# Routed experts on 37 token tiles instead of 38: two shared tiles divided at 96

## The chip, the cores and the metric

The kernel runs on one core of one Trainium2 chip. The metric is the device time of one execution in microseconds (us); lower is better. A core has TensorE (PE; PEld is its weight load), VectorE (DVE), ScalarE (ACT), GpSimd (POOL) and a queue for plain transfers (SP). They run side by side and wait for each other by semaphores.

## The reference

Two blocks in a row, all in fp32: sliding attention, and a layer of 8 experts in which each token goes to one expert. Cut to what matters here:

```python
B, H, S, Dh = 8, 8, 576, 64          # 8 x 576 = 4608 tokens, D = 8 x 64 = 512
E, F = 8, 1024                       # 8 experts, hidden width 1024
attn = softmax(mask(q @ k.T / sqrt(Dh))) @ v          # window 32; half the heads dilated by 4
x = attn.transpose(0, 2, 1, 3).reshape(B, S, 512)
logits = x @ w_gate                                   # [B, S, 8]
local  = sigmoid(x @ w_local)
for b in range(B):
    for s in range(S):
        fresh = argmax(logits[b, s])
        e = fresh if s == 0 or local[b, s] < 0.5 else prev_e    # keep the expert of the token before
        prev_e = e
        h = relu(x[b, s] @ w1[e])                     # w1[e]: 512 x 1024, the first product
        out[b, s] = softmax(logits[b, s])[e] * (h @ w2[e])      # w2[e]: 1024 x 512, the second; times the gate
```

Which tokens an expert gets is known only at run time. The kernel computes each expert on its own tokens alone, gathered into tiles of 128.

## The kernel before

The first 137 us or so are attention; the router's work lies in its gaps. Once the first two of four groups of two batches are routed, 11 early tiles are formed from whole 128s of an expert; when all four are routed, the rest. 4608 tokens are 36 tiles of 128, but no expert has a multiple of 128: the remainder of an expert goes into a whole tile of its own if it is over 64, and into half of a shared tile if not. A shared tile has two positions, so two experts' weights. Three extra tiles run only if the counts ask for it.

```python
CAP = N // P                       # 4608 / 128 = 36
HALF = P // 2
EARLY = -(-(GROUPS[0] * GS - E * (P - 1)) // P)           # 11
FULL, MIXED, EXTRA = CAP - EARLY, 2, 3                    # 25 plain late tiles, 2 shared, 3 extra
# order: 11 early, a shared one, 25 plain (two chains of experts in turn), the other shared one; extras
...
# table(), the late part: which expert gets how many tiles and where its remainder begins
nc.vector.tensor_scalar(big, rest, float(HALF), None, Alu.is_gt)
nc.vector.scalar_tensor_tensor(small, rest, 0.0, big, Alu.is_gt, Alu.subtract)
...
def hidden(t, half):               # first product: h = relu(w1.T x), four of eight blocks m at a time
    hp = bank([P, FK // 2, P], "hp")
    to = by_half(hp, 1)[:, 0]
    for m in range(FK // 2):
        at = half * FK // 2 + m
        if len(ps) > 1:            # a shared tile: 64 weight columns by 64 tokens
            for swap in range(2):
                for kk in range(DK):
                    for u, p in enumerate(ps):
                        h = (u + swap) % 2 * HALF
                        nc.tensor.matmul(to[h:h + HALF, u, m], lhsT=w1s[p % 2][:, at, kk, h:h + HALF],     # L901
                                         rhs=x[:, kk, u * HALF:(u + 1) * HALF], ..., tile_position=(0, h))
        else:
            for kk in range(DK):
                nc.tensor.matmul(hp[:, m], lhsT=w1s[ps[0] % 2][:, at, kk], rhs=x[:, kk], ...)              # L907
    nc.scalar.activation(ht[t][:, half * FK // 2:(half + 1) * FK // 2], hp, Act.Relu)                      # L911

def output(t):                     # second product, and the gate
    yp = bank([P, D], "yp")
    for m in range(FK):
        if len(ps) > 1:
            for u, p in enumerate(ps):
                nc.tensor.matmul(yp[u * HALF:(u + 1) * HALF], lhsT=halves[:, m // (FK // 2), u, m % (FK // 2)],  # L931
                                 rhs=w2s[p % 2][:, m], ..., tile_position=(0, u * HALF))
        else:
            nc.tensor.matmul(yp, lhsT=h[:, m], rhs=w2s[ps[0] % 2][:, m], ...)                              # L935
        if go and m % 2 == 0:
            gather(t + 3, m // 2)  # tokens of the tile after next but one, by GpSimd (L860)
    y = mp.tile([P, D], F32, name="y")
    nc.vector.tensor_scalar(y, yp, of_tile("gate", t), None, Alu.mult)                                     # L943
    nc.gpsimd.indirect_dma_start(out=out, ..., in_=y)                                                      # L944

def weights(t, second, c):         # a quarter (512 KB) of w1 or w2 of a position, left out if the buffer
    cond = {} if t < 2 else dict(cond=ev[t] != ev[t - 2], cond_hint=False)      # already has this expert
    nc.sync.dma_start(out=s[t % 2][:, c * m:(c + 1) * m], in_=w[ev[t], c], **cond)
```

There are two buffers of weights, taken in turn by position. Between the first and the second product of a tile, TensorE transposes the gathered tokens of the next one (L877), and DVE copies them from PSUM (L879). `put` (L770) are products that turn the places of the tokens into the list of each tile; pv (L429) and sc (L376) are attention's, lp (L481) is the router's. Between matmuls, calls of `gap` (cut here) let waiting steps of the router and the list-making be put into TensorE's order.

Of the kernel before, what the change touches and what calls it, by code (L numbers as in the profile page):

```python
# [69 lines left out]

GROUPS = (2, NG)
EARLY = -(-(GROUPS[0] * GS - E * (P - 1)) // P)
FULL, MIXED, EXTRA = CAP - EARLY, 2, 3
COLS = (EARLY, FULL + MIXED + EXTRA)


# [18 lines left out]
C_ROW = C_GO + E * (NJ + 1)  # L97
C_AT = C_ROW + EARLY + FULL + 2 * MIXED + EXTRA
C_NUM = C_AT + FULL + 2 * MIXED + EXTRA
C_PAY = C_NUM + P  # L100
C_ALL = C_PAY + NG * NJ * TW


def plan():


    tiles = [[0, i // 2 + i % 2 * (EARLY - EARLY // 2), 1] for i in range(EARLY)]
    tiles += [[1, FULL, 2]]
    tiles += [[1, i // 2 + i % 2 * (FULL - FULL // 2), 1] for i in range(FULL)]
    tiles += [[1, FULL + i, 2] for i in range(1, MIXED)]  # L110
    tiles += [[1, FULL + MIXED + i, 1] for i in range(EXTRA)]
    end = 0
    for tile in tiles:
        tile[2] = tuple(range(end, end + tile[2]))
        end = tile[2][-1] + 1
    return tiles
# [9 lines left out]
def constants():  # L126

    c = np.zeros((P, C_ALL), np.float32)
    c[:, C_ID:C_TRI] = np.eye(P)
    c[:TB, C_TRI:C_IDX] = np.triu(np.ones((TB, TB)), 1)  # L130
    c[:, C_IDX:C_REV] = np.arange(E)
    c[:, C_REV:C_CODE] = E - np.arange(E)
    c[:TB, C_CODE:C_GO] = (np.arange(NJ)[None] * TB + np.arange(TB)[:, None]) * CW + E
    c[:, C_GO:C_ROW] = (np.arange(E * (NJ + 1)) % (NJ + 1) > 0)

    for lv, col, ps in TILES:
        for u, p in enumerate(ps):
            c[:, C_ROW + p] = N if len(ps) > 1 else col - MIXED * (col > FULL)
            if lv:
                c[:, C_AT + p - EARLY] = col * P + u * HALF  # L140
    c[:, C_NUM:C_PAY] = np.arange(P)
    s = np.arange(NG * NJ)[None] * TB + np.arange(TB)[:, None]
    pay = np.zeros((TB, NG * NJ, TW), np.float32)
    pay[:, :, 0] = s - N
    at = s % S
    for w, at in ((2, at), (3, at % DIL * CI + at // DIL)):
        pay[:, :, w] = ((s // S * 2 + w - 2) * P + at % QB) * NB + at // QB - ROWS
    c[:TB, C_PAY:] = pay.reshape(TB, -1)
    return c
# [126 lines left out]
def whole(ctx, tc, exact, qk, v, wgl, w1, w2, con, msk, qmk, out, cst, wg, ones, xd, kept, register):  # L276
# [322 lines left out]
    def table(lv):  # L599
# [7 lines left out]
        def by_expert(name):  # L607
            return new([P, E], name)
# [7 lines left out]
        nc.vector.tensor_copy(full, ni)  # L616
        if late:

            rest, big, small = by_expert("rest"), by_expert("big"), by_expert("small")
            nc.vector.scalar_tensor_tensor(rest, full, -float(P), cn, Alu.mult, Alu.add)  # L620
            nc.vector.tensor_scalar(big, rest, float(HALF), None, Alu.is_gt)
            nc.vector.scalar_tensor_tensor(small, rest, 0.0, big, Alu.is_gt, Alu.subtract)
            full_then = by_expert("full_then")
            nc.vector.tensor_tensor(full_then, full, tiles["done"], op=Alu.subtract)
            nc.vector.tensor_tensor(full, full_then, big, op=Alu.add)
        end = by_expert("end")
        nc.vector.tensor_tensor_scan(end, full, full, 0.0, Alu.add, Alu.max)
        start = by_expert("start")
# [11 lines left out]
        if not late:  # L640
# [10 lines left out]
            return  # L651
        tiles["first", lv] = first = by_expert("first")
        nc.vector.tensor_scalar(first, tiles["done"], float(P), None, Alu.mult)

        upto, number = by_expert("upto"), by_expert("number")
        nc.vector.tensor_tensor_scan(upto, small, small, 0.0, Alu.add, Alu.max)
        nc.vector.tensor_tensor(number, upto, small, op=Alu.subtract)
        total = end[:, E - 1:]
        nc.vector.tensor_scalar(number, number, total, None, Alu.add)
        most = new([P, 1], "most")  # L660
        nc.vector.tensor_scalar(most, total, float(FULL), None, Alu.max)
        half, begin = by_expert("half"), by_expert("begin")
        nc.vector.tensor_scalar(half, number, most, None, Alu.subtract)

        nc.vector.tensor_scalar(begin, half, float(HALF), float(FULL * P), Alu.mult, Alu.add)
        nc.vector.tensor_scalar(number, number, float(P), None, Alu.mult)
        nc.vector.tensor_tensor(begin, begin, number, op=Alu.min)
        nc.vector.tensor_scalar(half, half, 2.0 * MIXED, None, Alu.is_ge)
        nc.vector.scalar_tensor_tensor(number, number, -float(MIXED * P), begin, Alu.add, Alu.subtract)
        nc.vector.tensor_tensor(number, number, half, op=Alu.mult)  # L670
        nc.vector.tensor_tensor(begin, begin, number, op=Alu.add)

        nc.vector.tensor_scalar(full_then, full_then, float(P), None, Alu.mult)
        tiles["off_half", lv], tiles["from", lv] = off_half, since = by_expert("off_half"), by_expert("since")
# [2 lines left out]
        nc.vector.tensor_tensor(since, since, full_then, op=Alu.add)  # L677

        nc.vector.tensor_tensor(small, small, cst[:, C_IDX:C_REV], op=Alu.mult)
        nc.vector.tensor_tensor(ge, begin[0:1].unsqueeze(1).to_broadcast(shape),  # L680
                                cst[0:1, C_AT:C_AT + nt].unsqueeze(2).to_broadcast(shape), op=Alu.is_equal)
        nc.vector.tensor_tensor(ge, ge, small[0:1].unsqueeze(1).to_broadcast(shape), op=Alu.mult)
# [2 lines left out]
        none = new([1, nt], "none")  # L685
        nc.vector.tensor_scalar(none, er, float(E), -float(E), Alu.is_ge, Alu.mult)
        nc.vector.tensor_tensor(er, er, none, op=Alu.add)
        nc.vector.tensor_tensor(experts, er, eh, op=Alu.add)

        over, all_tiles = new([1, 1], "over"), new([1, 1], "all_tiles")  # L690
        nc.vector.tensor_tensor(over, total[0:1], upto[0:1, E - 1:], op=Alu.add)
        nc.vector.tensor_tensor(over, over, most[0:1], op=Alu.subtract)
        nc.vector.tensor_scalar(over, over, -2.0 * MIXED, 0.0, Alu.add, Alu.max)
        nc.vector.tensor_tensor(all_tiles, over, most[0:1], op=Alu.add)
        nc.vector.tensor_scalar(kept["number"], all_tiles, float(LAST - FULL), None, Alu.add)
        known[0] = POS

# [47 lines left out]
    def mark(lv, g):  # L745

        nt = COLS[lv]
        by_place = marks.tile([TB, NJ, P], F32, name="by_place")
        shape = [TB, NJ, P]
        nc.vector.tensor_tensor(by_place, cst[:TB, C_NUM:C_PAY].unsqueeze(1).to_broadcast(shape),  # L750
                                tiles["place"][:, g].unsqueeze(2).to_broadcast(shape), op=Alu.is_equal)
        shape = [TB, NJ, nt]
        there = sm.tile([TB, NJ, max(COLS)], F32, name="there")[:, :, :nt]
        nc.vector.tensor_tensor(there, cst[:TB, C_NUM:C_NUM + nt].unsqueeze(1).to_broadcast(shape),
                                tiles["tile"][:, g].unsqueeze(2).to_broadcast(shape), op=Alu.is_equal)
        by_tile = marks.tile([TB, NJ, loads(lv), nt], F32, name="by_tile", tag="by_tile", bufs=1)
        for w in range(loads(lv)):
            nc.vector.tensor_tensor(by_tile[:, :, w], there, pay[:, g, :, w].unsqueeze(2).to_broadcast(shape),
                                    op=Alu.mult)
        tiles["marks"] = by_place, by_tile  # L760
# [122 lines left out]

    def hidden(t, half):

        x, ps = xe[t], TILES[t][2]
        if not half:
            ht[t] = mp.tile([P, FK, P], F32, name="h")
        for p in ps:
# [2 lines left out]
        to = by_half(hp, 1)[:, 0]  # L892
        for m in range(FK // 2):
            at = half * FK // 2 + m
            if len(ps) > 1:

                for swap in range(2):
                    for kk in range(DK):
                        for u, p in enumerate(ps):
                            h = (u + swap) % 2 * HALF  # L900
                            here[:] = [nc.tensor.matmul(  # L901
                                to[h:h + HALF, u, m], lhsT=w1s[p % 2][:, at, kk, h:h + HALF],
                                rhs=x[:, kk, u * HALF:(u + 1) * HALF], start=(kk == 0), stop=(kk == DK - 1),
                                tile_position=(0, h), skip_group_check=True)]
            else:
                for kk in range(DK):
                    here[:] = [nc.tensor.matmul(hp[:, m], lhsT=w1s[ps[0] % 2][:, at, kk], rhs=x[:, kk],  # L907
                                                start=(kk == 0), stop=(kk == DK - 1))]
            if m < FK // 2 - 1:
                gap(0.9)  # L910
        nc.scalar.activation(ht[t][:, half * FK // 2:(half + 1) * FK // 2], hp, Act.Relu)  # L911
        if half:
            hid.update(ps)
            fetch(at_once[0])

    def by_half(h, n):

        return h.rearrange("p m q -> p (m q)").rearrange("p (a u m q) -> p a u m q", a=n, u=2, q=HALF)

    def output(t):  # L920
# [4 lines left out]
        go = t + 3 < min(LAST, named[0]) and not any(a <= t + 3 < a + 3 for a in (0, EARLY))  # L925
        halves = by_half(h, 2)
        for m in range(FK):
            if len(ps) > 1:

                for u, p in enumerate(ps):  # L930
                    here[:] = [nc.tensor.matmul(yp[u * HALF:(u + 1) * HALF], lhsT=halves[:, m // (FK // 2), u, m % (FK // 2)], rhs=w2s[p % 2][:, m],  # L931
                                                start=(m == 0), stop=(m == FK - 1), tile_position=(0, u * HALF),
# [7 lines left out]
            else:  # L940
                gap(0.9)
        y = mp.tile([P, D], F32, name="y")
        nc.vector.tensor_scalar(y, yp, of_tile("gate", t), None, Alu.mult)  # L943
        nc.gpsimd.indirect_dma_start(  # L944
            out=out, out_offset=bass.IndirectOffsetOnAxis(ap=of_tile("tok", t), axis=0),
            in_=y, in_offset=None, bounds_check=N - 1, oob_is_err=False)
# [15 lines left out]
    def route(g):  # L962
# [4 lines left out]
        lv = GROUPS.index(g + 1) if g + 1 in GROUPS else None  # L967
        if lv is not None:
            steps.insert(5, (0.0, lambda g: table(lv)))
            steps.append((1.2, lambda g: seek(lv)))  # L970

        waiting.extend((us if g + 1 == GROUPS[0] else 2 * us, lambda f=f: f(g)) for us, f in steps)
# [149 lines left out]
```

## Time and profile before

| | |
|---|---|
| time, three executions | 719.64 us median; 718.02 and 1607.11 the others |
| profiled execution | 713.95 us, span 712.2 us, granted TensorE clock 0.995 |
| tiles of the experts | 38: 36 plain, 2 shared |
| first and second product of plain tiles (L907, L935) | 265.0 and 255.0 us busy |
| first and second product of shared tiles (L901, L931) | 15.7 and 14.2 us busy |
| gathers (L860), two kinds of 76 | 973 and 948 ns on GpSimd on the mean, 2.7 us to landing (median) |

The span is what the profile covers, from the first to the last instruction of one execution; the time is of other executions and takes in a little more. An "x" gives the number of records; one fp32 matmul leaves two of them, each with its weight load. The chain of work that ended last is followed back from the last instruction: each piece is what the next one waited for.

```profile
L860 POOL DMA_INDIRECT xg<-xd,plain x76 | 74.0, 973 | 290.1 <-PE yp L935 243.9
L911 ACT ACTIVATE h<-hp 128x512 f32<-128x512 f32 x76 | 45.4, 597 | 499.6 <-PE hp L907 471.6
L943 DVE TENSOR_SCALAR y<-yp,gate 128x512 f32<-128x512 f32 x38 | 28.5, 751 | 212.1 <-DMA xg<-xd,dilated 92.7
```

A line of the groups has the source line, engine, operation, tile written and read, and count; then the busy time in us and the mean of one in ns; then how long the engine stood idle before it, and for whom.

### The profile page before, as it was taken

How to read it: one execution, taken by the hardware profiler on the slowest of the kernel's cores; microseconds unless marked ns; L12 is line 12 of the kernel's file. 1: busy time of each engine (PE TensorE's matmuls, PEld its weight loads, DVE VectorE, ACT ScalarE, POOL GpSimd, SP SyncE). 2: the span in 40 equal slices, each digit the busy share in tenths (PEclk: the TensorE clock that was granted, in tenths of full speed). 3: DMA queues.
4: the chain of work that ended last, by engine and by line, in shares of the span. 5: the costliest groups of instructions: out<-in, count | busy, mean ns of one | idle time of the engine just before them, and what ended most of it. 6: DMA issues, size and time to landing. Idle time of an engine off the chain costs nothing.

```text
span 712.2 us, 16720 instructions
## 1 busy us (share of the span) xinstructions
PE 695.4 (98%) x6460; PEld 527.5 (74%) x6460; DVE 194.8 (27%) x554; ACT 125.1 (18%) x241; POOL 211.2 (30%) x219
## 2 busy tenths in 40 slices
PE   8999989999999999999999999999999999999995
PEld 6989788876777777776677767776777667776772
DVE  4668797632257221001010101010100101010100
ACT  3565545412110000110001100110000000110010
POOL 2322200542223335203332333223332333233100
PEclk9999999999999999999999999999999999999998
DMA  9989779931864842807692451811178117201780
GB/s 340 384 278 341 244 265 396 392 139 31 295 237 148 287 136 53 273 25 260 197 319 72 134 170 38 270 38 34 38 256 291 35 37 240 73 31 38 228 295 15
DMA packets 37591, 131.24 MB, mean 184 GB/s; under 512 B 6686, under 2 KB 6814, under 8 KB 37504
## 3 DMA queue, kind: packets, MB, share of 16 engines
q1 hardware_dynamic: 29600, 110.68, 43.6%
q0 software_dynamic: 7904, 19.41, 9.7%
q8 instruction: 53, 0.87, 0.5%
q14 instruction: 34, 0.28, 0.1%
HBM read 207.37 MB, written 19.69 MB: 319 GB/s over the span
## 4 chain that ended last, share of the span: by engine, by line
PE 94%; DVE 4%; ACT 1%; issue 0%; POOL 0%; POOLq 0%; DVEq 0%
PE hp L907 36%; PE yp L935 35%; PE sc L376 6%; PE pv L429 4%; PE tp L877 2%; PE tp L455 2%; PE hp L901 2%; PE yp L931 2%; DVE pr L383 1%; PE lp L481 1%; PE put L770 1%; PE idle L341 1%; DVE x L435 1%; ACT pr L386 0%; ACT xt L466 0%
## 5 line engine op out<-in xcount | busy, mean ns | idle before, releaser
L907 PEld LDWEIGHTS hp<-xe,w1s 128*128 128x128 f32 x2304 | 263.3, 192 | 18.3 <-issue 16.3
L907 PE MATMUL hp<-xe,w1s 128*128 128x128 f32 x2304 | 265.0, 276 | 1.3 <-DVE xe L879 1.3
L935 PE MATMUL yp<-w2s,h 128*128 128x512 f32 x576 | 255.0, 594 | 0.0
L935 PEld LDWEIGHTS yp<-w2s,h 128*128 128x128 f32 x576 | 106.2, 190 | 118.0 <-issue 117.6
L860 POOL DMA_INDIRECT xg<-xd,plain x76 | 74.0, 973 | 290.1 <-PE yp L935 243.9
L911 ACT ACTIVATE h<-hp 128x512 f32<-128x512 f32 x76 | 45.4, 597 | 499.6 <-PE hp L907 471.6
L860 POOL DMA_INDIRECT xg<-xd,dilated x76 | 72.1, 948 | 57.1 <-PE yp L935 51.4
L943 DVE TENSOR_SCALAR y<-yp,gate 128x512 f32<-128x512 f32 x38 | 28.5, 751 | 212.1 <-DMA xg<-xd,dilated 92.7
L879 DVE COPY xe<-tp 128x512 f32<-128x512 f32 x38 | 26.2, 690 | 216.8 <-PE tp L877 216.8
L944 POOL DMA_INDIRECT out_dram<-y,tok x38 | 38.9, 1022 | 79.8 <-DVE y L943 78.8
L376 PE MATMUL sc<-kq 64*96 64x64 f32 x1152 | 57.2, 248 | 3.2 <-DVE pr L383 2.0
L376 PEld LDWEIGHTS sc<-kq 64*96 64x96 f32 x1152 | 52.2, 162 | 6.7 <-DVE pr L383 2.2
L383 DVE SCALAR_TENSOR_TENSOR pr<-sc,mk 96x640 f32<-96x640 f32 x64 | 47.8, 749 | 26.8 <-PE pv L429 15.6
L386 ACT ACTIVATE pr<-pr 96x640 f32<-96x640 f32 x64 | 43.6, 684 | 53.9 <-DVE pr L383 51.2
L332 POOL COPY vt<-vt 32x1040 f32<-32x1040 f32 x25 | 26.1, 1045 | 67.7 <-DMA vt<-in_v_dram 57.5
L429 PE MATMUL pv<-vt,pr 96*64 96x65 f32 x1152 | 43.6, 227 | 0.5 <-ACT xt L466 0.5
L429 PEld LDWEIGHTS pv<-vt,pr 96*64 96x64 f32 x1152 | 37.7, 139 | 6.5 <-issue 3.0
L435 DVE TENSOR_TENSOR x<-pv,rec 128x320 f32<-128x320 f32 x64 | 27.0, 454 | 0.2
L877 PE MATMUL tp<-cst,xg 128*128 128x128 f32 x152 | 23.0, 274 | 0.0
L455 PE MATMUL tp<-cst,x 128*128 128x128 f32 x144 | 20.3, 288 | 1.5 <-DVE x L435 1.4
L466 ACT COPY xt<-tp 128x288 f32<-128x288 f32 (+2 forms) x48 | 18.3, 557 | 1.9 <-PE tp L455 1.7
L455 PEld LDWEIGHTS tp<-cst,x 128*128 128x128 f32 x144 | 16.3, 146 | 2.7 <-DVE x L435 1.8
(178 smaller groups left out, 223.5 us busy)
## 6 DMA issues: line engine op xcount, KB each, us to landing
w1s<-in_w_dram SPq DMA_DIRECT2D x160, 512.0 KB
w2s<-in_w_dram SPq DMA_DIRECT2D x160, 512.0 KB
kq<-in_qk_dram SPq DMA_DIRECT2D x32, 592.0 KB
vt<-in_v_dram SPq DMA_DIRECT2D x32, 292.5 KB
xd<-x SPq DMA_DIRECT2D x16, 576.0 KB
xg<-xd,plain POOLq DMA_INDIRECT x76, 2.7
xg<-xd,dilated POOLq DMA_INDIRECT x76, 2.7
out_dram<-y,tok POOLq DMA_INDIRECT x38, 4.7
```

The costliest lines, as they stand in the source:

```text
L376: here[:] = [nc.tensor.matmul(sc[:KW, u, (i - a) * QB:(i - a + 1) * QB], lhsT=kt[h, i * QB:i * QB + KW], rhs=qt[h, i * QB:(i + 1) * QB], s ...
L383: nc.vector.scalar_tensor_tensor(pr[:, :, :w], sc[:KW, :, :w], -CEIL, mk[:, at:at + w].unsqueeze(1).to_broadcast([KW, 2, w]), Alu.max, Alu ...
L386: nc.scalar.activation(pr[:, :, :w], pr[:, :, :w], Act.Exp, scale=SCALE)
L429: here[:] = [nc.tensor.matmul(pv[u * QB:(u + 1) * QB, i - a], lhsT=pr[:, u, (i - a) * QB:(i - a + 1) * QB], rhs=vt[:, u, i], start=True, s ...
L435: nc.vector.tensor_tensor(x[:, a:z, n % 2], pv[:, :, :DH], r.unsqueeze(2).to_broadcast([P, z - a, DH]), op=Alu.mult)
L455: nc.tensor.transpose(tp[:, :, i], x[:, c * w + i].rearrange("p g d -> p (g d)"), ident)
L860: i = nc.gpsimd.indirect_dma_start(out=xg[t][:, kk], out_offset=None, in_=xd if full == ROWS else xd[:full], in_offset=bass.IndirectOffset ...
L877: nc.tensor.transpose(tp[:, kk], x[:, kk], ident)
L907: here[:] = [nc.tensor.matmul(hp[:, m], lhsT=w1s[ps[0] % 2][:, at, kk], rhs=x[:, kk], start=(kk == 0), stop=(kk == DK - 1))]
L911: nc.scalar.activation(ht[t][:, half * FK // 2:(half + 1) * FK // 2], hp, Act.Relu)
L935: here[:] = [nc.tensor.matmul(yp, lhsT=h[:, m], rhs=w2s[ps[0] % 2][:, m], start=(m == 0), stop=(m == FK - 1))]
L944: nc.gpsimd.indirect_dma_start(out=out, out_offset=bass.IndirectOffsetOnAxis(ap=of_tile("tok", t), axis=0), in_=y, in_offset=None, bounds_ ...
```

## The change

It packs the remainders closer. A remainder takes a whole tile only if it is over 96. There are three shared tiles, two of them divided at 96 (a part of 96 tokens and one of 32), one at 64; a remainder goes into the smallest kind of part that holds it, or a larger one if those are used up. 23 plain late tiles are left, so 11 + 23 + 3 = 37. A new step `parts` works out on DVE which part each expert gets. One 96-tile follows the early tiles, the other stands in the middle of the plain ones, the tile divided at 64 at the end.

In a 96-tile the first product goes in column halves: 64 weight columns by 96 tokens of one expert, then 64 by 32 of the other. The second goes in four column quarters of 32 tokens, three with one expert's weights and one with the other's. The gate of the last tile is halved between DVE and ACT. The space in SBUF for the list of GpSimd's transfers goes from 4096 to 1024 bytes of a partition.

```diff
+SPLITS = (96, 96, 64)
+SIZES, PARTS = (96, 64, 32), (2, 2, 2)
+K = len(SIZES)
+MIXED, EXTRA = len(SPLITS), 3
+FULL = CAP - EARLY - 2
...
-    tiles += [[1, i // 2 + i % 2 * (FULL - FULL // 2), 1] for i in range(FULL)]
-    tiles += [[1, FULL + i, 2] for i in range(1, MIXED)]
+    full = [[1, i // 2 + i % 2 * (FULL - FULL // 2), 1] for i in range(FULL)]
+    for i in range(1, MIXED):
+        a, z = ((i + k - 1) * FULL // (MIXED - 1) for k in range(2))
+        tiles += full[a:z] + [[1, FULL + i, 2]]
...
+            more = new([P, K + 1, E], "more")
+            nc.vector.tensor_tensor(more, rest.unsqueeze(1).to_broadcast([P, K + 1, E]),
+                                    cst[:, C_SIZE:C_UPTO].unsqueeze(2).to_broadcast([P, K + 1, E]), op=Alu.is_gt)
...   # and the new step parts(lv): order of the parts, where each begins, the experts of the positions
...
-            if len(ps) > 1:
+            if at_96:
+                for p, a, z in ((ps[0], 0, SPLITS[0]), (ps[1], SPLITS[0], P)):
+                    for kk in range(DK):
+                        for h in (0, HALF):
+                            here[:] = [nc.tensor.matmul(
+                                hp[h:h + HALF, m, a:z], lhsT=w1s[p % 2][:, at, kk, h:h + HALF], rhs=x[:, kk, a:z],
+                                start=(kk == 0), stop=(kk == DK - 1), tile_position=(0, h), skip_group_check=True)]
+            elif len(ps) > 1:
...
+            if split(t) == SPLITS[0]:
+                for a in range(0, P, P // 4):
+                    here[:] = [nc.tensor.matmul(yp[a:a + P // 4], lhsT=h[:, m, a:a + P // 4],
+                                                rhs=w2s[ps[a >= SPLITS[0]] % 2][:, m], start=(m == 0), stop=(m == FK - 1),
+                                                tile_position=(0, a), skip_group_check=True)]
+            elif len(ps) > 1:
...
-        nc.vector.tensor_scalar(y, yp, of_tile("gate", t), None, Alu.mult)
+        half = D // 2 if t == LAST - 1 else D
+        nc.vector.tensor_scalar(y[:, :half], yp[:, :half], of_tile("gate", t), None, Alu.mult)
+        if half < D:
+            nc.scalar.activation(y[:, half:], yp[:, half:], Act.Copy, scale=of_tile("gate", t))
...
+            if lv:
+                steps.insert(6, (0.7, lambda g: parts(lv)))
...
-    nc = _bacc.Bacc("TRN2", target_bir_lowering=False, num_devices=1, dynamic_dma_scratch_size=4096)
+    nc = _bacc.Bacc("TRN2", target_bir_lowering=False, num_devices=1, dynamic_dma_scratch_size=1024)
```

## The prediction

> **What bounds the kernel now.** I read the page's table of busy time first, then the chain that ended last in order of time, then the groups with shapes kept apart.
>
> ```profile
> PE 695.4 (98%) x6460; PEld 527.5 (74%) x6460; DVE 194.8 (27%) x554; ACT 125.1 (18%) x241; POOL 211.2 (30%) x219
> ```
>
> TensorE is busy for 695.4 of 712.2 us; no other engine passes 30%. A busy PE isn't proof of a full one, so the chain has to show what follows what:
>
> ```profile
> 297.65 7.14 PE hp L907 x64
> 305.23 6.87 PE yp L935 x16
> 312.10 7.62 PE hp L901 x256
> 320.30 7.02 PE yp L931 x32
> 327.32 7.34 PE hp L907 x64
> 335.10 6.87 PE yp L935 x16
> 341.96 7.15 PE hp L907 x64
> ...
> 689.08 5.63 PE hp L901 x186
> 694.96 2.25 PE hp L901 x69
> 697.21 6.96 PE yp L931 x31
> 704.19 0.76 DVE y L943
> 705.48 0.72 POOL out_dram L944
> ```
>
> The columns are start, length, what, and the number of matmul records (an fp32 matmul leaves two). From about 265 us the chain is nothing but first products (hp) and second products (yp), with some 0.44 us between them for the four transposes of the next tile. So a plain tile costs 7.14 + 0.44 + 6.87 = 14.45 us, and the starts agree: 312.10 - 297.65 = 14.45. The one shared tile in the middle (L901 and L931) costs 327.32 - 312.10 = 15.22. No weight, gather or vector work stands in the chain between tiles: the time falls only if TensorE gets less to do. Each tile removed is worth a whole tile.
>
> **What the Trainium skill says.** (1) "TensorEngine Tiling (Array Packing)", Key Properties: column tiles load weights and multiply independently, and a change of mode drains the array. The trace agrees: halves give 32 records of 512 columns in 7.02 us where the whole array needs 6.87 for 16, so two run at once. For quarters there is the router's product (L481), which already uses four column groups with four different moving operands:
>
> ```profile
> 110.60 2.17 PE lp L481 x31
> ```
>
> One of its records streams 288 columns. From yp, one record of 512 columns takes 6.87/16 = 429 ns, so 288 columns take 242 ns. Its 32 records (31 are in the trace) in 2.17 us are 68 ns each, hence 3.6 at a time: four quarters do run together. (2) "TensorE: Matmul & The Clock Gate", Wait — 56ns, not 53.3ns?: starts never come closer than about 25 ns, however few columns move. (3) the same page, LDWEIGHTS: a weight load's time goes with its columns, not with its rows. The trace shows both, with a somewhat higher floor:
>
> ```profile
> 52.35 1.20 PE pv L429 x36
> 53.55 1.68 PE sc L376 x36
> ...
> 113.39 1.03 PE put L770 x36
> 225.19 1.20 PE put L770 x36
> ```
>
> The rows sc load 96 columns and move 64; 1.68/36 is 47 ns each. The rows pv load 64 and move 65; 33 ns. More weight columns at the same moving width cost more. The rows put load 64 columns and move 44 in the first case, 60 in the second: 29 to 33 ns, although by width they should differ by a quarter. So with 64 weight columns there is a floor of about 30 ns a record, under which narrower moving operands gain nothing. L901, 64 columns by 64, has 7.62/256 = 29.8 ns and sits on it too. (4) "DMA: Bandwidth & Descriptors", SWDGE vs HWDGE vs iDMA: GpSimd appends descriptors to rings in SBUF, which the DMA engines drain. The "list 1 KB" makes these shorter; no run yet shows what a short one costs.
>
> **The change, part by part.** *Which tiles.* I counted tokens by expert from the reference's inputs. The remainders after whole tiles of 128 are 11, 94, 31, 107, 20, 58, 87 and 104. Before, 107, 104, 94 and 87 take a whole tile each, and the four small ones fill two tiles in halves: 11 early + 25 + 2 = 38. After, only 107 and 104 need a whole tile; 94 and 87 take the 96-slots, 58 and 11 the halves, 31 and 20 the 32-slots: 11 + 23 + 3 = 37, with no spare tile. Against before, two plain tiles and a half-and-half tile go (2 x 14.45 + 15.22 = 44.12 us), and two tiles divided at 96 come. The third shared tile stays a half-and-half one at the end, as before.
>
> *First product of a 96-tile.* 256 records again, all with 64 weight columns: 128 move 96 columns and 128 move 32. By width a whole-array record of 128 columns takes 7.14/64 = 112 ns; two halves at once with 96 columns make 112 x 0.75 / 2 = 42 ns each, above the floor: 128 x 42 = 5.4 us. With 32 columns width would give 14 ns, but the floor of 30 holds: 128 x 30 = 3.8 us. Together 9.2 us, where the even halves took 7.62. I leave the loads that could run ahead at each turn from 96 to 32 out of the sum.
>
> *Second product.* 64 records of 512 columns, four at a time: 64 x 429 / 4 = 6.86 us, and with the start-up of about 0.2 to 0.4 that halves (7.02) and the router show, 7.15 us. All tokens of a tile go through together, so this costs almost nothing against 6.87.
>
> *Sum of a 96-tile:* 9.2 + 0.55 for transposes and mode changes (0.58 between L901 and L931 now) + 7.15 = 16.9 us, two of them 33.8.
>
> *Last gate.* DVE's last pass takes 0.75 us for 512 columns (0.76 in the chain). Halved, DVE takes about 0.45; ACT's copies of 96, 192 and 288 columns in L488 take 0.23, 0.31 and 0.39, so 256 should take 0.37, beside DVE. This is on the path: -0.3 us.
>
> *List-making on DVE.* The order of instructions shows seven more small operations in the late table, 0.15 to 0.2 us each, 1.2 us in all, and an added step moves the put products eight matmuls later in TensorE's order (about 0.9 us). In the trace the first put's marks are done at 223.3 and the put starts at 225.19: 1.9 us of slack. Cost 0.
>
> *Weights.* Positions 11, 13 and 14 now load around the first shared tile, where before only 11 and 14 did (13 kept its expert). Loads start as each quarter of the old weights is used up. The run into the last tile shows how fast that goes: four loads of 2 MB, issued from 662 to 689 us, moved at about 300 GB/s, 7 us each, with only the gap at 694.7 above for TensorE. Counted from the start of the first 96-tile, w1 of 13 would land by 11, w1 of 14 by 18, w2 of 13 between 20 and 25, where its quarters are needed from 24.4 to 29.8. The second 96-tile needs one load, as both neighbours keep expert 6 in one buffer. Cost 0, with a risk of 1 to 2 us.
>
> *Sum:* -44.1 + 33.8 - 0.3 = -10.6 us, 1.5% of 719.64: 709.0 us.
>
> **The rivals.** *A, the narrow records are hidden.* If weight loads of the 32-column part run ahead under the 96-column part, the first product is no worse than an even half tile, 7.62. Each 96-tile then costs 15.3, the change brings 13.8, and the time is 706. Against it: put and pv, which show the floor in streams that have nothing narrow to hide behind, and PEld, which L901 already keeps busy without a pause:
>
> ```profile
> L901 PEld LDWEIGHTS hp<-xe,w1s 128*64 128x64 f32 x512 | 15.3, 138 | 1.9 <-issue 1.9
> ```
>
> *B, quarters don't run four at a time.* Four streams of 512 columns for 7 us are more than the router's 288 for 2 us. At two at a time, the second product takes twice 6.86 us, and each 96-tile 9.2 + 0.55 + 13.7 = 23.5; then 47.0 comes for the 44.1 and 0.3 that go, 2.6 us more than before: 722 us. The router's 3.6 speaks against it; at 3 at a time the loss per tile is 2 us, and the time 713.
>
> *C, a wait takes its place.* Gathers could wait for room in the shorter list, or the extra load arrive late. GpSimd has 30% of busy time, one gather every 1.7 us, landing after a median 2.7 us; at most two or three are under way, and I expect no wait. If every output of a tile waited for the list, TensorE would still have three tiles of gathers ahead of it. 710 to 712 us.
>
> **Range and chances.** The removed 44.1 us is sure as long as the routing is as I counted; the term with doubt is the first product of the 96-tiles, 7.7 to 9.8 us, twice (-3.0 to +1.2), then quarters (0 to +2 each) and single microseconds of waits. That gives some 705.5 to 714. The times before differ from each other by 1.6 us (718.02 and 719.64), and the profiled one is lower still, 713.95, so a run of the changed kernel may land low: 704.5 to 713. Faster by 2% needs -14.4 us, which is rival A at its best or the luck of a run; slower by 2% needs spare tiles or quarters that run one by one: faster 0.12, same 0.85, slower 0.03.
>
> **What would show it.** In the profile after: 37 tiles in the chain; two pieces of 256 hp records of some 9.2 us (right if 8.9 to 9.6; rival A if under 8); two pieces of 64 yp records of 7.0 to 7.4 us (rival B if 9 or more); the plain tile still 14.45 us apart; two last gate passes side by side, each under 0.5 us; gathers still near 0.95 us and landing in about 2.7. The prediction is wrong if spare tiles run after the last gate, if TensorE stands still around the first 96-tile, or if gathers lengthen.

## The result and the profile after

The changed kernel takes 706.59 us (median; 705.59 to 707.14) where the kernel before took 719.64: a ratio of 0.9824 with a 95% interval of 0.9802 to 0.9847. In a second session it took 704.03 against 715.78, ratio 0.983 (0.9809 to 0.985). That is 11 to 14 us less; 10.6 were predicted.

TensorE's busy time fell with the span, and nothing else became the bound (the page's first part, changed kernel):

```profile
PE 688.0 (98%) x6648; PEld 520.5 (74%) x6648; DVE 194.3 (28%) x559; ACT 124.8 (18%) x240; POOL 206.4 (29%) x214
```

The chain that ended last is of no use here: in this trace it runs back through GpSimd's outputs and gaps called "issue". The timeline of TensorE shows the same tiles instead: start, length, line, what, number of records. The first 96-tile of the changed kernel:

```profile
302.41 7.31 PE L963 MATMUL hp<-xe,w1s 128*128 128x128 f32 x64
309.56 0.60 PE L925 MATMUL tp<-cst,xg 128*128 128x128 f32 x4
309.99 7.03 PE L1000 MATMUL yp<-w2s,h 128*128 128x512 f32 x16
316.95 9.21 PE L948 MATMUL hp<-xe,w1s 128*64 128x96 f32 x256
326.09 0.66 PE L925 MATMUL tp<-cst,xg 128*128 128x128 f32 x4
326.68 7.07 PE L991 MATMUL yp<-w2s,h 128*32 128x512 f32 x64
333.68 7.41 PE L963 MATMUL hp<-xe,w1s 128*128 128x128 f32 x64
```

Lengths overlap a little, so starts are subtracted. The 96-tile takes 333.68 - 316.95 = 16.73 us: 9.14 for the first product, 0.59 for the transposes, 7.00 for the second. TensorE has no gap around it. (x256 in L948 stands for both shapes, 96 and 32 tokens.)

The end of the changed kernel, from the last tile's second product on:

```profile
691.21 7.05 PE L996 MATMUL yp<-w2s,h 128*64 128x512 f32 x32
...
698.32 0.48 DVE L1010 TENSOR_SCALAR y<-yp,gate 128x256 f32<-128x256 f32 x1 [13.98 <-PE yp L996]
698.83 0.47 ACT L1012 ACTIVATE y<-yp,gate 128x256 f32<-128x256 f32 x1 [6.81 <-DVE y L1010]
699.82 1.00 POOL L1013 DMA_INDIRECT out_dram<-y,tok  x1 [13.99 <-ACT y L1012]
```

The bracket names the idle time before and what ended it: ACT waited for DVE. The two halves of the last gate run one after the other, which was not foreseen. From the issue on GpSimd to the end of the span there are 5.5 us; the kernel before has 712.2 - 705.22 = 7.0.

Cut in stages at the same events (us, from the traces; a tile begins with its first product, and the end is where the span ends):

| trace | first expert product begins | from there to the first shared tile | shared tile | first shared to last tile | last tile to issue of its output | issue to end |
|---|---|---|---|---|---|---|
| before | 138.78 | 173.25 | 15.22 | 376.98 | 16.21 | 7.0 |
| before_again | 141.23 | 173.26 | 15.22 | 376.98 | 15.66 | 7.0 |
| list_1k | 140.59 | 173.26 | 15.22 | 376.98 | 16.62 | 5.4 |
| changed | 141.67 | 175.28 | 16.73 | 366.52 | 16.35 | 5.5 |
| again | 145.11 | 173.20 | 16.73 | 366.52 | 16.10 | 5.4 |
| gate_dve | 139.90 | 173.19 | 16.72 | 366.51 | 15.87 | 5.5 |
| two_banks | 140.44 | 173.20 | 16.73 | 366.52 | 15.63 | 5.9 |
| list_3k | 140.54 | 173.21 | 16.72 | 367.37 | 15.87 | 6.3 |

The columns from the first product to the last tile hardly move from run to run, so they can be compared to a tenth of a microsecond. The first column can't: it lies between 138.8 and 147.9 in all traces, with either kernel. A single profile's span therefore says little about a change of 10 us; the stages do. (175.28 in one trace is a first tile begun at half the TensorE clock, 0.51 granted from 141.6 to 145.1 us, after an idle time of 1.7 us; it came once.)

### The profile page after: what moved, and what is told of

Same layout as the page of the kernel before. It is cut to its first block, busy times and chain, and to the rows that moved or that the text cites. A ratio compares the mean times of both kernels' runs of the same rounds, so it can differ in the third digit from the quotient of the medians.

```text
span 705.4 us, 17078 instructions
## 1 busy us (share of the span) xinstructions
PE 688.0 (98%) x6648; PEld 520.5 (74%) x6648; DVE 194.3 (28%) x559; ACT 124.8 (18%) x240; POOL 206.4 (29%) x214
## 5 line engine op out<-in xcount | busy, mean ns | idle before, releaser
L963 PEld LDWEIGHTS hp<-xe,w1s 128*128 128x128 f32 x2176 | 250.2, 193 | 17.8 <-issue 15.3
L963 PE MATMUL hp<-xe,w1s 128*128 128x128 f32 x2176 | 252.1, 276 | 1.7 <-DVE xe L927 1.7
L1000 PE MATMUL yp<-w2s,h 128*128 128x512 f32 x544 | 240.6, 593 | 0.0
L1000 PEld LDWEIGHTS yp<-w2s,h 128*128 128x128 f32 x544 | 100.2, 190 | 111.8 <-issue 111.5
L908 POOL DMA_INDIRECT xg<-xd,plain x74 | 72.1, 975 | 286.8 <-PE yp L1000 226.6
L908 POOL DMA_INDIRECT xg<-xd,dilated x74 | 70.2, 949 | 58.3 <-PE yp L1000 38.0
L1010 DVE TENSOR_SCALAR y<-yp,gate 128x512 f32<-128x512 f32 (+1 forms) x37 | 27.5, 743 | 206.8 <-PE yp L1000 180.0
L948 PEld LDWEIGHTS hp<-xe,w1s 128*64 128x64 f32 x512 | 18.2, 137 | 1.5 <-issue 1.5
```

The source lines that it names most:

```text
L908: i = nc.gpsimd.indirect_dma_start(out=xg[t][:, kk], out_offset=None, in_=xd if full == ROWS else xd[:full], in_offset=bass.IndirectOffset ...
L1000: here[:] = [nc.tensor.matmul(yp, lhsT=h[:, m], rhs=w2s[ps[0] % 2][:, m], start=(m == 0), stop=(m == FK - 1))]
L1010: nc.vector.tensor_scalar(y[:, :half], yp[:, :half], of_tile("gate", t), None, Alu.mult)
```

## The experiments

Two questions were open. Why does the first product of a 96-tile take 9.1 us and not the 7.6 of even halves: is there a fixed time between starts, a weight load, or can it be hidden? And why is the end behind the last issue 1.5 us shorter, which the tiles don't explain?

**again.** The changed kernel, unedited.

> The changed kernel once more, beside the kernel before on the same chip, to size the change and to see whether the first 140 us differ. If the whole gain lies in the experts' tiles, from the first shared tile to the end it takes 388 us again where the kernel before took 400, and the time is 11 to 12 us under the kernel before, plus whatever the attention phase adds by chance. If the change also does something to the attention phase, the start of the first expert tile is shifted by some microseconds in each run.

Measured: 704.03 us, 0.983 (0.9809 to 0.985) of the kernel before. From the first shared tile to the end 706.3 - 318.31 = 388.0 us, as foreseen, against 400.2 and 399.6 in the two traces of the kernel before: -11.9 on the mean. The start of the first expert product moved by 3.4 us against the first trace of the same kernel. The gain lies in the tiles and behind them; in what precedes, two traces of one kernel differ by as much as the kernels do.

**narrow_twice.** In the first product:

```diff
-                for p, a, z in ((ps[0], 0, SPLITS[0]), (ps[1], SPLITS[0], P)):
+                for p, a, z in ((ps[0], 0, SPLITS[0]), (ps[1], SPLITS[0], P), (ps[1], SPLITS[0], P)):
```

> The 32-column part of the first product is computed twice in both 96-tiles (same result). Floor theory: a record with 64 weight columns costs about 30 ns however few columns move, so 128 more records cost 3.8 us in each tile: the first product of a 96-tile goes from 9.2 to 13.0, the time 7.7 us up. Width theory (the 32-column part costs its width, 14 ns a record, and the 1.5 us over an even tile come from changing between widths): 1.8 us in each tile, the time 3.6 us up.

Measured: 712.06 us, 8.0 over *again*. The timeline of TensorE:

```profile
321.15 12.94 PE L948 MATMUL hp<-xe,w1s 128*64 128x96 f32 x384
334.02 0.66 PE L925 MATMUL tp<-cst,xg 128*128 128x128 f32 x4
```

The first product went from 9.14 to 334.02 - 321.15 = 12.87 us; 3.73 us for 128 more records are 29 ns each, twice what 32 tokens should take by width. The width theory is out.

**interleaved.** Wide records of one half of the array beside narrow ones of the other:

```diff
-                for p, a, z in ((ps[0], 0, SPLITS[0]), (ps[1], SPLITS[0], P)):
-                    for kk in range(DK):
-                        for h in (0, HALF):
+                wide, narrow = (ps[0], 0, SPLITS[0]), (ps[1], SPLITS[0], P)
+                for kk in range(DK):
+                    for h, (p, a, z) in ((0, wide), (HALF, narrow), (HALF, wide), (0, narrow)):
```

> In the 96-tiles the 32-column records of one half of the array are put beside the 96-column ones of the other half. If the floor is the weight load, and it can run while the other half streams, 256 records at 30 ns take 7.7 us, and what must start in order keeps it at 8.0 to 8.6: the time 1 to 2.5 us under the changed kernel. If every narrow record costs its 30 ns of TensorE wherever it stands, the first product stays at 9.1 to 9.3 and the time the same.

This order opens the sums of the wide and the narrow part at the same time in the same bank and partitions. The Trainium skill, "PSUM — Partial Sum Buffer", The four PSUM rules, says that the second sum's first product then clears the marks of the first, so the 96-tiles don't hold the reference's sums here; the marks show in no trace, and only the time is read. Measured: 702.81 us, and in the trace the first 96-tile takes 16.76 us where the changed kernel has 16.73; its first product has 9.24 where that has 9.21. Nothing was hidden in this order. So the 1.2 us by which the time is lower are not the tile's doing; they are within what the start-up varies by. Rival A found no support; another order wasn't tried.

**whole_array.** The first product of the 96-tiles without column halves:

```diff
-                        for h in (0, HALF):
-                            here[:] = [nc.tensor.matmul(
-                                hp[h:h + HALF, m, a:z], lhsT=w1s[p % 2][:, at, kk, h:h + HALF], rhs=x[:, kk, a:z],
+                        here[:] = [nc.tensor.matmul(
+                            hp[:, m, a:z], lhsT=w1s[p % 2][:, at, kk], rhs=x[:, kk, a:z],
```

> The first product of the 96-tiles without column halves: 128 weight columns by 96 tokens, then by 32. 64 records at 0.75 of 112 ns are 5.4 us, and 64 narrow ones are bound by a load of 128 columns, about twice the 30 ns of 64: 3.8 us; 9.2 in all, the same as in halves: the halving of the first product is worth nothing. If instead two halves at once are what keeps the narrow part cheap, the narrow part takes longer than 3.8 us, and the time goes up by 1 us or more.

Measured: 712.41 us, 8.4 over *again*. I had expected no change. The timeline of TensorE, and below it the groups with shapes kept apart:

```profile
312.03 14.38 PE L947 MATMUL hp<-xe,w1s 128*128 128x96 f32 x128
326.24 0.64 PE L925 MATMUL tp<-cst,xg 128*128 128x128 f32 x4
```

```profile
L947 PEld LDWEIGHTS hp<-xe,w1s 128*128 128x128 f32 x256 | 28.9, 192 | 1.0 <-issue 1.0
L947 PE MATMUL hp<-xe,w1s 128*128 128x96 f32 x128 | 17.6, 280 | 0.0
L947 PE MATMUL hp<-xe,w1s 128*128 128x32 f32 x128 | 16.1, 269 | 0.0
```

128 records took 326.24 - 312.03 = 14.21 us, 111 ns each, and the plain tile's records of 128 tokens take 112. So 96 and 32 tokens cost what 128 cost; the starts of the single records say the same, 112 ns from one to the next in either part. I had given the wide records 84 ns by their width. (That PEld is busy all the time is no evidence: it is so in the changed kernel too, 9.10 of 9.14 us.) What fits is that a record isn't shorter than the load of the weights for the next one, some 0.87 ns for each weight column (111 / 128). In halves, the changed kernel starts two records 7 ns apart, one in each half, and the next two 59 ns after the first two with 32 tokens, 83 with 96: that is 64 weight columns (56 ns) in one case and 96 tokens (84) in the other. Halving the columns halves the load and runs two loads at once: the column halves are what makes a 96-tile cheap, 5.1 us a tile. (Two tiles make 10.0 us in the trace; the medians, 8.4 apart, have the start-up in them.)

**narrow_64.** The narrow part first, with 64 tokens, then the wide part over it:

```diff
-                for p, a, z in ((ps[0], 0, SPLITS[0]), (ps[1], SPLITS[0], P)):
+                for p, a, z in ((ps[1], HALF, P), (ps[0], 0, SPLITS[0])):
```

> The narrow part of the first product comes first and moves 64 tokens instead of 32; the 96-column part then writes over the 32 that aren't the narrow expert's, so that the result stays. The number of records and of weight columns is that of the changed kernel. Weight-load theory (a record takes the longer of its weight columns and its tokens): 64 tokens by 64 weight columns take what 32 by 64 take, about 30 ns, and the first product of a 96-tile stays at 9.1 to 9.3 us, the time with it. If the narrow part costs by its tokens plus a fixed amount, twice the tokens add 13 ns a record, 1.7 us in each tile, and the time goes up by 3.4 us.

Measured: 703.45 us, 0.9816 (0.9756 to 0.9876). The timeline of TensorE:

```profile
312.19 9.23 PE L948 MATMUL hp<-xe,w1s 128*64 128x64 f32 x256
321.36 0.66 PE L925 MATMUL tp<-cst,xg 128*128 128x128 f32 x4
```

Twice the tokens in the narrow part cost 9.17 - 9.14 = 0.03 us (the order of the two parts changed with them). Together with *whole_array* this settles it: with 64 weight columns, 32 and 64 tokens cost the same.

**narrow_quarters.** The narrow part in four column quarters:

```diff
-                for p, a, z in ((ps[0], 0, SPLITS[0]), (ps[1], SPLITS[0], P)):
+                for p, a, z, w in ((ps[0], 0, SPLITS[0], HALF), (ps[1], SPLITS[0], P, P // 4)):
                     for kk in range(DK):
-                        for h in (0, HALF):
+                        for h in range(0, P, w):          # and h:h + w in the slices
```

> The 32-column part of the first product in four column quarters instead of two halves: twice as many records, each with 32 weight columns. The whole-array run gave 112 ns a record for 32, 96 and 128 tokens alike, so a record takes the longer of its weight columns and its tokens, about 0.87 ns a column with what is around it. By that a quarter's record takes 28 ns, four at once 7 ns each, and 256 of them 1.8 us instead of 3.8: the first product of a 96-tile 7.1 to 7.3 us, the time 4 us shorter. If there is a floor between starts that doesn't depend on columns, some 25 ns as the 30 ns of halves would allow, they take 6.4 us, and the time is 5 us longer.

Measured: 708.82 us, 0.9897 (0.9849 to 0.9945). By the weight columns alone it would have been faster. The first products of its two 96-tiles on the timeline of TensorE:

```profile
315.80 8.81 PE L948 MATMUL hp<-xe,w1s 128*64 128x96 f32 x340
325.45 1.10 PE L948 MATMUL hp<-xe,w1s 128*64 128x96 f32 x44 [0.84 <-issue]
...
493.54 5.86 PE L948 MATMUL hp<-xe,w1s 128*64 128x96 f32 x212
500.25 3.16 PE L948 MATMUL hp<-xe,w1s 128*32 128x32 f32 x128 [0.85 <-issue]
503.71 1.10 PE L948 MATMUL hp<-xe,w1s 128*64 128x96 f32 x44 [0.29 <-issue]
```

From the first shared to the last tile it takes 370.13 us where the changed kernel takes 366.52: 3.6 us more. Three pauses called "issue", in which TensorE waited for nothing that the profile names, account for 2.7 of these (1.06, 1.09 and 0.51 from start to start, the records before them running out included). The starts of the single records tell the rest. Within the narrow part, four quarters start 7, 7, 6 and 12 ns after one another: 32 ns for four, 8 ns a record, so the weight columns do count as expected (7). What I had left out is the change between halves and quarters. From the last wide record to the first quarter 176 ns pass where the changed kernel has 76, and on the way back 126 instead of 52. So a narrow part with its way back falls only from 437 to 388 ns, and a wide part with its way out grows from 690 to 811: 0.07 us lost in a block, where the quarters alone would have won 0.2 (16 x 29 ns less 32 x 8). With eight blocks in a tile, the last without a way back, that is some 0.5 a tile, which is what the pauses leave.

The pauses have a likely cause in the same trace. A queue of the DMA called "instruction" brings packets of 16384 bytes; there are 53 of them in *whole_array*, 55 in the changed kernel and 57 here and in *narrow_twice*, so one goes with 128 records more of TensorE. Each of the three pauses ends 1.3 to 1.5 us after such a packet has landed, and the records at which two of them stand in one tile, after 212 and after 340, are 128 apart. Between them 128 records ran in 3.17 us, and packets came 3.3 to 3.9 us apart in these tiles: TensorE seems to have used up its instructions faster than they came. No run tested this.

**gate_dve.** The last gate as it was:

```diff
-        half = D // 2 if t == LAST - 1 else D
-        nc.vector.tensor_scalar(y[:, :half], yp[:, :half], of_tile("gate", t), None, Alu.mult)
-        if half < D:
-            nc.scalar.activation(y[:, half:], yp[:, half:], Act.Copy, scale=of_tile("gate", t))
+        nc.vector.tensor_scalar(y, yp, of_tile("gate", t), None, Alu.mult)
```

> The changed kernel with the last gate by DVE alone. In the changed kernel ACT begins its half only when DVE has ended (0.48, then 0.47 us, 1.5 us from the first to the issue of the output, where the kernel before has 1.03). If the two passes are in series, undoing the part makes the time 0.4 to 0.5 us shorter. If they overlapped in truth and only the trace shows them apart, 0.3 us longer.

Measured: 702.57 us, 0.9824 (0.9783 to 0.9864); such an interval can't show 0.3 us, the trace can:

```profile
694.20 0.75 DVE L1009 TENSOR_SCALAR y<-yp,gate 128x512 f32<-128x512 f32 x1 [13.74 <-PE yp L996]
695.47 1.00 POOL L1010 DMA_INDIRECT out_dram<-y,tok  x1 [13.51 <-DVE y L1009]
```

From the first gate pass to the issue 1.27 us; the changed kernel has 699.82 - 698.32 = 1.50. Undoing the part shortens the end by 0.2.

**two_banks.** The last second product in two halves of 256 columns, in banks of their own:

```diff
+        yp = bank([P, D // 2], "yp_left") if end else bank([P, D], "yp")
+        yr = bank([P, D // 2], "yp_right") if end else None
...
+        for c, yh in enumerate((yp, yr) if end else ()):
+            for m in range(FK):           # as before, into yh, with columns c * 256 to (c + 1) * 256 of w2
...
+            nc.scalar.activation(y[:, half:], yr, Act.Copy, scale=of_tile("gate", t))
```

> The changed kernel with the last second product in two column halves of 256 that lie in two banks, one after the other, so that DVE and ACT read different banks. If the shared bank holds ACT back, ACT's pass no longer waits for DVE's, DVE's half runs under the second half's products, and the time from the last product to the issue of the output falls from 1.6 us to about 0.7: 0.9 us shorter than the changed kernel, unless shorter products cost TensorE some of it (32 records more of 256 columns instead of 32 of 512: at most 0.2 us). If something else orders the two passes, they stay in series.

Measured: 703.21 us, 0.9814 (0.9776 to 0.9852). The end of its trace:

```profile
693.72 1.03 PE L992 MATMUL yp_right<-w2s,h 128*64 128x256 f32 x8
694.80 0.47 ACT L1021 ACTIVATE y<-yp_right,gate 128x256 f32<-128x256 f32 x1 [6.31 <-PE yp_right L992]
695.79 1.00 POOL L1022 DMA_INDIRECT out_dram<-y,tok  x1 [13.27 <-ACT y L1021]
```

ACT now waits for its own product instead of DVE, whose pass was over by 691.8. From the last pass's start to the issue 0.99 us, half a microsecond less than the changed kernel; 0.9 were expected, because I left out the half microsecond between ACT's end and the issue, which stays. The two passes still write the same tile y in SBUF, but that isn't what orders them: the trace has ACT past its wait for DVE's semaphore at 688.1, before DVE's pass began at 691.3. What held ACT back was the shared bank, or the one PSUM tile in it: two tiles in one bank weren't tried. The Trainium skill says why, "PSUM — Partial Sum Buffer", PSUM bank collisions raise a hardware error: two engines must not touch the same bank in the same partitions at once, reads among reads included, and the hardware doesn't keep them apart, so the program has to put the two in order. In the changed kernel it does: ACT waits for DVE's semaphore. I had not looked that up for the last gate.

**list_1k.** The kernel before with `dynamic_dma_scratch_size=1024` in place of 4096.

> The kernel before with the list of 1024 bytes and nothing else of the change. From the issue of the last output (on GpSimd) to the end of the span the kernel before takes 7.0 us, and all kernels with the short list so far 5.4 to 5.6. If the list makes that difference, this kernel ends 5.4 to 5.6 us after that issue, and its time is 1 to 1.5 us under the kernel before. If the list costs nothing and brings nothing, both stay, and the shorter end must come from the tiles or the last gate. If room in the list were short, gathers would take longer than 0.97 us or land late.

Measured: 715.48 us against 715.14, 0.9989 (0.9966 to 1.0012): no difference that this can show, and -1.2 us lies inside. In the trace the end takes 5.4 us instead of 7.0, but the last output is issued 1.27 us after the gate's start instead of 1.03. Gathers are the same length and hardly land later: 967 and 949 ns on GpSimd, 2.8 us to landing at the median over both kinds.

**list_3k.** The changed kernel with 3072 bytes.

> The changed kernel with a list of 3072 bytes instead of 1024 (4096 don't fit beside its other buffers). With 4096 the one trace of the kernel before ends 7.0 us after the issue of the last output, with 1024 every trace so far 5.4 to 5.8. If the end goes with the list's length, 3072 bytes end about 6.5 us after the issue; if it doesn't, 5.4 to 5.8 again. The time itself moves by at most 1 us.

Measured: 704.3 us, 0.9818 (0.9758 to 0.9878). The issue is at 696.99 and the span ends at 703.3: 6.3 us. Its 0.85 us more between the first shared and the last tile are a pause inside the second 96-tile, 0.67 us long, after 212 of its 256 records. *interleaved* has one of 0.58 at the same record, and the kernel before has them too, in the last shared tile after 186 records: 0.25 us in its first trace, 0.42 in *list_1k*. All are of the "issue" kind, and all end 1.3 to 1.5 us after a packet of instructions landed, as in *narrow_quarters*; in the traces without a pause at these places, the packet had landed 1.36 us or more before. A weight that comes late would hardly keep to a count of records. The last output is issued 1.27 us after the gate's start where the changed kernel has 1.50, so the delay of the issue comes with 1024 bytes and not with 3072.

**before_again.** The kernel before, unedited.

> The kernel before, unchanged, for a second trace of it. From the first shared tile to the start of the last tile it takes 377.0 us again, as twice so far. If its 7.0 us from the last issue to the end belong to the list of 4096 bytes, they come again; if they were chance, 5.4 to 5.8. The start of the first expert tile lies anywhere from 138 to 148 us, as in the other traces, whatever the kernel.

Measured: 715.58 us against 715.78, 0.9992 (0.9964 to 1.002). 376.98 us from shared tile to last tile, and 714.1 - 707.13 = 7.0 to the end. So the end goes with the list: 7.0 and 7.0 us with 4096 bytes, 6.3 with 3072, 5.4 to 5.9 in ten traces with 1024. The records of GpSimd's sequencer (POOLq) show where. At the program's end stands a DRAIN, the longest of three; first the kernel before, then *list_3k*, then the changed kernel (least, median and greatest length in ns):

```profile
L1118 POOLq DRAIN  x3: 40/107/1863, 709.5 to 711.9; - x3
L1189 POOLq DRAIN  x3: 40/107/1455, 701.0 to 703.1; - x3
L1189 POOLq DRAIN  x3: 40/107/638, 703.8 to 705.1; - x3
```

Together with the instruction ahead of it (INC_SWDGE_SEM) it takes 2.53 us with 4096 bytes, 2.02 with 3072 and 1.00 with 1024, the same in all traces of a size: 0.51 us for each 1024 bytes of list.

## Why the prediction was right, and where not

*The tiles carry the gain: right.* 37 tiles ran and no spare one. Predicted from the first shared tile to the last -44.1 + 33.8 = -10.3 us, measured 366.52 - 376.98 = -10.46. Most plain tiles still start 14.45 us apart (the rest 14.54 to 14.66, as before).

*A 96-tile at 16.9 us: right, 16.73.* The first product at 9.2 is 9.14, the second at 7.15 is 7.00, transposes at 0.55 are 0.59. Four quarters do run at once: 64 records of 429 ns in 7.00 us are 3.9 at a time. Rival B is out.

*The floor: right in size, wrong in kind.* "With 64 weight columns there is a floor of about 30 ns" held (29), and so did the two terms of the sum: the wide parts take 8 x 0.69 = 5.5 us (5.4 predicted), the narrow ones 8 x 0.44 = 3.5 (3.8). But the text took the Trainium skill's 25 ns between starts as its support, and worked the wide part out from the tokens' width. *whole_array* and *narrow_64* show that the floor is the weight load, which goes with the weight columns: 111 ns for 128, 29 ns a record for 64 in two halves at once; *narrow_quarters* has 8 ns for 32 in four quarters, well under 25. The wide part came out right since 96 tokens are more than 64 columns. Where the step would have gone wrong is the whole array, where I expected no change and got 8.4 us. Of the places in the Trainium skill on this, LDWEIGHTS was the one that decides, and the row sc with its 47 ns had said so.

*Rival A, hidden narrow records: no.* 9.24 in the one order tried.

*List-making and weights at 0: right.* From the first expert product to the first shared tile 173.25 us before, 173.20 after; no pause at either 96-tile in the changed kernel. The pause of 0.6 us in the second, in two of the other traces, goes with the arrival of instructions, and so does the gap at 694.7 in the kernel before that the prediction set beside the loads.

*The last gate at -0.3: wrong.* The step that failed is the one that put ACT's half "beside DVE": the halves run in series on one bank, and ACT's takes 0.47 us and not 0.37. Against DVE alone with the same list it costs 0.23 us (1.50 for 1.27).

*The list at 0: wrong in the other direction.* I asked only whether a short list makes gathers wait. It doesn't, but it shortens the end by 1.5 us and delays the last issue by 0.24. One sign that I had named did fail: gathers were to land in about 2.7 us, and in *again* the medians are 4.3 and 4.5 for those whose landing the trace gives, with their length on GpSimd unchanged (949 ns for one kind). The list isn't the reason (2.7 and 3.1 in *list_1k*, 4.3 and 2.6 in *list_3k*); the reason is open. It cost nothing: TensorE's idle time ahead of the transposes of gathered tokens is 0.0 us in both traces of the changed kernel. So rival C didn't come about.

*The sum.* -10.46 for the tiles, -1.5 for the end, and some +0.3 between the last tile's start and its issue (16.35 and 16.10 against 16.21 and 15.66) make -11.7. (The last gate and the list alone would make it +0.5; the 16.21 has one of the pauses in it.) The -11.7 lie in both measured intervals, 719.64 x 0.0153 to 0.0198 = 11.0 to 14.2 and 10.7 to 13.7; the predicted 10.6 lies at their edge. What the medians may have beyond 11.7 can't be told from the chance of the first 140 us. Outside the tiles 10.6 owes something to luck: the term of -0.3 had the wrong sign, and the -1.5 of the end wasn't in the sum.

## What to carry to other kernels

Where TensorE has no gaps, work saved there is time saved, and its size can be read from the distance between two starts in the trace; to check such a gain, compare the stage and not the span, whose start-up may vary by more than the gain. When matmuls are cut into parts, ask of each record which is longer, its tokens or the weight columns that must be loaded for the next: narrowing the tokens below the weight columns saves nothing, narrowing the columns does, until the change between the ways of cutting costs more than it saves. Splitting a pass between two engines helps only if each has a bank of its own.

## What was not expected of the hardware

- fp32 records with 128 weight columns take 111 ns for 32, 96 or 128 tokens alike; in column halves 29 ns for 32 or 64 tokens; in quarters with 32 weight columns and 32 tokens 8 ns. A change from halves to quarters takes 176 ns from start to start and one back 126, where a change of width alone takes 76 and 52.
- TensorE paused seven times in five traces from the first shared tile on, for 0.25 to 0.85 us, with nothing named that it waited for. Each pause ended 1.3 to 1.5 us after a packet of 16384 bytes had landed in the DMA's queue for instructions.
- The time from the last output's issue to the end of the program goes with the space for GpSimd's list: 5.4 to 5.9 us with 1024 bytes, 6.3 with 3072, 7.0 with 4096. The last DRAIN on GpSimd takes 0.64, 1.46 and 1.86 us.
- DVE took 0.48 us for half of the last tile's columns where it takes 0.75 for all, so a halved pass is worth 0.27 us at best.
